# Earlier row gathers and weighings, and map products behind the value gates, in an attention and mixture-of-experts kernel

## The chip, the cores and the metric

The kernel runs on one core of one Trainium2 chip. A core has five engines with their own in-order instruction streams: PE (TensorE, matrix products; its weight loads are shown apart as PEld), DVE (VectorE), ACT (ScalarE), POOL (GpSimd) and SP (SyncE, which here only issues transfers). The metric is the device time of one execution in microseconds (us); three runs of the kernel before gave 779.08, 781.21 and 781.72 us.

## The reference

Three stages follow each other on 4 x 576 = 2304 tokens with 8 heads of 64 features.

```python
# 1 linear attention with random features, per batch and head
def phi(x):
    proj = x @ w_phi                                   # 64 -> 128
    proj = proj - max(abs(proj), axis=-1)
    return concatenate([exp(proj), exp(-proj)])        # 256 features
kv  = phi(k)^T @ v ;  z = sum(phi(k))
x   = (phi(q) @ kv) / (phi(q) @ z + 1e-6)              # -> 2304 x 512
# 2 mixture of experts, top 1 of 8, at most 576 tokens each
idx = argmax(x @ w_gate) ;  gate = softmax(x @ w_gate)[idx]
y   = relu(x[token] @ w1[e]) @ w2[e] ;  x = gate * y   # 512 -> 1024 -> 512
# 3 one dense layer on all tokens
h   = x @ w_in ;  out = (h - tanh(h)) @ w_out          # 512 -> 2048 -> 512
```

A token that finds its expert full gives a row of zeros.

## The kernel before

**Attention** works in 25 steps `s` on 18 chunks of 128 tokens. In a step the keys of chunk `s` are projected, the products of keys and values of chunk `s-1` are added (`kv_step`, PE line 347), the queries of chunk `s-5` are projected (PE line 304 into `xb`), and the outputs of an earlier chunk are formed (`num`, PE line 420). `sub` is on DVE: it takes the largest absolute value (line 312) and subtracts it (line 315); as `xb` serves keys and queries in turn, the next projection waits for line 315. `vgate` (PE line 334, result in the PSUM tile `sb`, copied by ACT at line 338) makes the part of the expert logits that comes from the values. Beside this, 13 pieces of the dense layer's weights are unpacked on ACT, DVE (lines 92 and 94) and POOL (lines 98 and 278).

**Routing** goes by groups of three chunks. `since[cs]` is the number of steps since the group's last chunk had its output formed. For the first four groups (`paced`) one step does `route1`, the next its rest, the third `prefix`, `route2` and `table`, and the fourth the products of the map: `map_mm` (PE line 576) multiplies two small tables, `ta` from DVE (line 558) and `tb` from POOL (line 548), into another part of `sb`, and `map_add` (DVE lines 581 and 583) adds them to `idc`. From `idc` the lists of rows that each expert gets are made at the end of attention.

**Experts and dense layer** work in units of 576 tokens; a unit is one expert that has tokens, and in these data three units are run. A unit has 8 steps through the expert (`ff1`, `ff2`) and then 16 steps through the dense layer: two blocks `b` of 288 tokens, eight pieces of 256 hidden features each. A dense step `s` is, on PE, `ffin` of step `s` (24 products) and `ffout` of step `s-2` (24 products). The nonlinearity (`gate`) stands between: ACT copies `ffin`'s PSUM tile `h` to `hs` (line 938) and squares it, POOL makes a mask (line 943) in the tile `AL` that `ffout` of step `s-2` still reads, DVE does the rest (lines 947 to 955, then line 931 for the low part). There is one `hs`, two tiles `h` and two `AL`.

In the dense steps of a unit the rows of the next unit are fetched. `xgather` clears one of three tiles `row` on POOL (line 860) and issues an indirect transfer from POOL's queue (line 861); `weigh` multiplies the row by its attention denominators on POOL (line 872); `xsplit` at the start of steps 8, 9 and 10 transposes it on PE (line 881, four products) and splits it into high and low parts on ACT and DVE (lines 849 and 850). Steps 11 to 13 have four transposes each too, of finished rows (`orow`, line 976). The third unit fetches for a fourth that is not run.

The order of every engine is the order in which the code is written (no scheduler moves it). In a dense step `xgather` and `weigh` come last, behind the mask of the same step:

```python
if 5 <= s <= 7:
    xgather(j + 1, s - 5)
...
if s in (7, 8, 9, 15):
    weigh()
```

Of the kernel before, what the change touches and what calls it, by code (L numbers as in the profile page):

```python
# [37 lines left out]
def build(nc, tc, ctx, qT, kT, vT, v, w_phi, w_gate, w12, win, wout, out, cap):  # L38
# [86 lines left out]
    def attention():  # L125
# [534 lines left out]
        for s in range(NCH + LAG + 2):  # L660
            i, j, jt = s, s - LAG, s - LAG - 1
            jn = jt if s < SD else jt - 1 if s > SD else -1
            kk, qq, tt = i < NCH, 0 <= j < NCH, 0 <= jt < NCH
            pc, pd = CV.get(s), CV.get(s - 1)
            since = {cs: s - (cs[-1] + LAG + 1 + (cs[-1] + LAG + 1 >= SD)) for cs in groups}
            if s == SK:
                stk.close()
                mo["alloc"]()
                qpools.append(st.enter_context(tc.tile_pool(name="qp2", bufs=1)))
            if kk:  # L670
                proj("k", i, xb if i > LAG or i % 2 == 0 else yb)
            if tt:
                trans(jt)
                qexp(jt, 0)
                qexp(jt, 1)
            if jn == NCH - 2:
                first_gather()
            for cs in maps:
                if since[cs] == 1 + 2 * (cs in paced):
                    prefix(cs)  # L680
                if since[cs] == 2 + 2 * (cs in paced) and cs in maps[:-1]:
                    map_mm(cs)
            if 0 <= i - 1 < NCH:
                kv_step(i - 1)
            if kk:
                for _ in sub("k", i):
                    pass
            bits = iter(()) if pc is None else cv_main(pc)
            next(bits, None)
            if qq:  # L690
                proj("q", j, xb)
            if i - 1 in strad:
                kv_second(i - 1)
            ke = kexp(i) if kk else iter(())
            next(ke, None)
            if pd is not None:
                cv_hi(pd)
                cv_lo(pd)
            for _ in ke:
                pass  # L700
            if qq:
                for _ in sub("q", j):
                    pass
            smalls = []
            for cs in groups:
                d = since[cs]
                if cs in paced:
                    if d == 1:
                        rgen[cs] = route1(cs)
                        smalls.append(itertools.islice(rgen[cs], 5))  # L710
                    if d == 2:
                        smalls.append(rgen[cs])
                    if d == 3:
                        smalls.append(itertools.chain(route2(cs), table(cs)))
                    if d == 4:
                        smalls.append(map_add(cs))
                elif cs in maps and d == 1:
                    smalls.append(itertools.chain(route2(cs), table(cs)))
            weave([], smalls)
            for _ in bits:  # L720
                pass
            flush()
            if 0 <= jn < NCH:
                num(jn)
            if kk:
                vgate(i)
            if CV.get(s + 1) is not None:
                cv_mag(CV[s + 1])
            for cs in groups:
                if cs not in paced and since[cs] == 0 and cs != tailg[1]:  # L730
                    weave([], [route1(cs)])
            if s + 2 < NCH:
                ldk(s + 2)
            if 0 <= j + 2 < NCH:
                ldq(j + 2)
            if pc is not None:
                cv_load(pc + NRAW)
            if s in (3, 4):
                cv_load(s - 3)
            if s + 2 < NCH:  # L740
                ldvt(s + 2)
            for c, a in vslot.get(s, []):
                if c > 1:
                    ldv(c, a)
            if 0 <= jn < NCH - NL:
                xstore([jn])
            for c in range(max(0, 4 * (s - NCH)), min(NCH, 4 * (s - NCH) + 4)):
                nc.sync.dma_start(out=out[c * P:(c + 1) * P, :].rearrange("t (a b) -> t a b", a=4),
                                  in_=zero.unsqueeze(1).to_broadcast([P, 4, P]))
            mo["after"](s)  # L750
            if jn == NCH - 2:
                xscale(NCH - 3)
# [40 lines left out]
    def experts():  # L793
# [277 lines left out]
        def unit(j, prev):  # L1071
# [64 lines left out]
            for s, (b, p) in enumerate(seq2):  # L1136
                if more and 8 <= s <= 10:
                    xsplit(s - 8)
                if 11 <= s <= 13:
                    orow(j, 0, s - 11)  # L1140
                h = ffin(b, p)
                if s == 0:
                    aq2[s] = gate(h)
                    ff2(aq.pop(n1 - 1), False, True)
                    evac_y(1)
                p2 = -1
                if s >= 2:
                    p2 = seq2[s - 2][1]
                    ffout(aq2.pop(s - 2), p2, p2 == 0, p2 == NP2 - 1)
                if s > 0:  # L1150
                    aq2[s] = gate(h, HALVES[:2] if s == n2 - 1 else HALVES[2:])
                if j == 0:

                    for k, f in enumerate(lord[LF:]):
                        if s == 2 * k:
                            late_load(f)
                        elif s == 2 * k + 1:
                            lbits[f] = late_bits(f)
                            next(lbits[f])
                            next(lbits[f])  # L1160
                        elif s == 2 * k + 2:
                            for _ in lbits[f]:
                                pass
                        elif s == 2 * k + 3:
                            late_split(f)
                if p2 == NP2 - 1:
                    evac_o(False)
                if more:
                    if s == 0:
                        use(j + 1)  # L1170
                        idload(j + 1, hs[:, 0])
                    if 5 <= s <= 7:
                        xgather(j + 1, s - 5)
                    if s == 3+WO:
                        wnext(0, 2)
                    if s == 4+WO:
                        wnext(1, 2)
                    if s == 5+WO:
                        wnext(0, 1)
                    if s == 6+WO:  # L1180
                        wnext(1, 1)
                    if s == 13:
                        xgather(j + 1, 3)
                    if s == 14:
                        xgather(j + 1, 4)
                    if s in (7, 8, 9, 15):
                        weigh()
            return [aq2[n2 - 2], aq2[n2 - 1]]

# [123 lines left out]
```

## Time and profile before

| | |
|---|---|
| runs (us) | 779.08, 781.21, 781.72 |
| the profiled execution (us) | 784.24, of which the span from first to last instruction is 782.5 |
| PE busy | 685.3 us (88%), 7148 products, mean granted clock 0.945 |
| DVE busy | 533.7 us (68%) |
| ACT busy | 431.0 us (55%) |
| POOL busy | 256.1 us (33%) |
| PE waits for `row` (line 872) before line 881 | 35.0 us in 9 |
| PE waits for `tb` and `ta` before line 576 | 12.3 us in 3, 6.9 us in 4 |

An engine's busy time says how much it worked, not whether it was waited for. The view of waits names for each idle stretch the instruction that ended it. The view by stretches gives every engine's busy time between two points of the span with PE's granted clock, where 1.00 is 2.4 GHz and half of it 1.2 GHz. In a timeline a row has its start, its duration, the instruction, and in brackets the engine's idle time ahead of it and what ended that.

### The profile page before, as it was taken

How to read it: one execution, taken by the hardware profiler on the slowest of the kernel's cores; microseconds unless marked ns; L12 is line 12 of the kernel's file. 1: busy time of each engine (PE TensorE's matmuls, PEld its weight loads, DVE VectorE, ACT ScalarE, POOL GpSimd, SP SyncE). 2: the span in 40 equal slices, each digit the busy share in tenths (PEclk: the TensorE clock that was granted, in tenths of full speed). 3: DMA queues.
4: the chain of work that ended last, by engine and by line, in shares of the span. 5: the costliest groups of instructions: out<-in, count | busy, mean ns of one | idle time of the engine just before them, and what ended most of it. 6: DMA issues, size and time to landing. Idle time of an engine off the chain costs nothing. (4 is left out here: it accounts for less than half of the span.)

```text
span 782.5 us, 17539 instructions
## 1 busy us (share of the span) xinstructions
PE 685.3 (88%) x7148; PEld 662.5 (85%) x7148; DVE 533.7 (68%) x830; ACT 431.0 (55%) x735; POOL 256.1 (33%) x227
## 2 busy tenths in 40 slices
PE   7899877967679999966999999976999999976995
PEld 6888767866569999966999999976999999976994
DVE  3689869657756767865986637745787636756783
ACT  2599767644544655644664536633664536634761
POOL 1044535342224233543461002433252002343351
PEclk9999989889968999989999999987999999989998
DMA  5987756626726630110223530000222440000111
GB/s 155 275 250 247 241 176 199 210 58 188 209 85 186 218 110 28 40 32 1 75 58 105 162 125 2 11 20 1 60 73 91 150 151 1 4 29 0 52 43 34
DMA packets 62155, 81.35 MB, mean 104 GB/s; under 512 B 25792, under 2 KB 35136, under 8 KB 60400
## 3 DMA queue, kind: packets, MB, share of 16 engines
q1 hardware_dynamic: 58736, 71.92, 29.7%
q0 software_dynamic: 2624, 8.13, 3.6%
q8 instruction: 58, 0.95, 0.5%
q14 instruction: 33, 0.27, 0.1%
q10 hardware_dynamic: 704, 0.08, 0.1%
HBM read 67.06 MB, written 13.05 MB: 102 GB/s over the span
## 5 line engine op out<-in xcount | busy, mean ns | idle before, releaser
L943 POOL TENSOR_SCALAR al<-ut 128x576 fp32r<-128x576 f32 (+1 forms) x51 | 83.1, 1629 | 200.1 <-ACT y L942 89.6
L853 PE MATMUL h<-xh,w_in_h 128*128 128x288 f32 x384 | 121.4, 316 | 0.0
L854 PE MATMUL h<-xl,w_in_h 128*128 128x288 f32 x384 | 118.9, 310 | 0.0
L855 PE MATMUL h<-xh,w_in_l 128*128 128x288 f32 x384 | 118.3, 308 | 0.0
L938 ACT COPY hs<-h 128x576 f32<-128x576 f32 (+1 forms) x51 | 31.3, 614 | 124.1 <-PE h L855 74.6
L840 DVE TENSOR_TENSOR w<-raw,w 128x512 fp32r<-128x512 f32 x98 | 67.8, 709 | 42.5 <-ACT w L835 34.7
L931 DVE TENSOR_TENSOR al<-y,ah 128x576 fp32r<-128x576 f32 (+1 forms) x51 | 38.1, 746 | 78.4 <-ACT ah L930 76.0
L835 ACT CAST w<-raw 128x512 fp32r<-128x512 f32 x98 | 58.9, 620 | 54.0 <-DMA raw<-w 22.0
L853 PEld LDWEIGHTS h<-xh,w_in_h 128*128 128x128 f32 x384 | 78.2, 204 | 0.0
L854 PEld LDWEIGHTS h<-xl,w_in_h 128*128 128x128 f32 x384 | 78.0, 203 | 0.0
L855 PEld LDWEIGHTS h<-xh,w_in_l 128*128 128x128 f32 x384 | 77.8, 203 | 0.0
L853 PE MATMUL acc<-ah,w_oa_h 128*128 128x288 f32 x240 | 71.0, 296 | 1.9 <-ACT ah L930 1.9
L854 PE MATMUL acc<-al,w_oa_h 128*128 128x288 f32 x240 | 71.1, 296 | 1.6 <-DVE al L931 1.6
L855 PE MATMUL acc<-ah,w_oa_l 128*128 128x288 f32 x240 | 70.7, 294 | 0.0
L312 DVE TENSOR_REDUCE m<-xb 128x8 f32<-128x1024 f32 x33 | 40.3, 1220 | 44.1 <-PE xb L304 44.1
L853 PE MATMUL h<-xh,w 128*128 128x288 f32 x192 | 58.9, 307 | 1.1 <-DVE al L899 1.1
L983 POOL DMA_INDIRECT out<-row,ids x18 | 20.8, 1154 | 118.7 <-DVE row L981 80.8
L347 PE MATMUL kvb<-v,kp 128*64 128x74 f32 x1280 | 53.2, 249 | 5.2 <-issue 3.1
L854 PE MATMUL h<-xl,w 128*128 128x288 f32 x192 | 57.5, 299 | 0.0
L855 PE MATMUL h<-xh,w 128*128 128x288 f32 x192 | 57.3, 299 | 0.0
L347 PEld LDWEIGHTS kvb<-v,kp 128*64 128x64 f32 x1280 | 50.0, 155 | 8.1 <-issue 4.8
L853 PE MATMUL acc<-ah,w 128*128 128x288 f32 x192 | 56.7, 295 | 0.0
(223 smaller groups left out, 1940.7 us busy)
## 6 DMA issues: line engine op xcount, KB each, us to landing
raw<-w SPq DMA_DIRECT2D x98, 256.0 KB, 2.8
raw<-win SPq DMA_DIRECT2D x8, 1024.0 KB, 7.1
raw<-wout SPq DMA_DIRECT2D x5, 1024.0 KB
k<-kT SPq DMA_DIRECT2D x18, 256.0 KB, 5.2
vt<-vT SPq DMA_DIRECT2D x18, 256.0 KB, 5.7
q<-qT SPq DMA_DIRECT2D x18, 256.0 KB, 2.5
out<-zero SPq DMA_DIRECT2D x18, 256.0 KB, 3.6
v<-v SPq DMA_DIRECT2D x16, 256.0 KB, 5.8
```

The lines of the kernel that those rows point to most:

```text
L312: nc.vector.tensor_reduce(out=m, in_=ps, axis=AX.X, op=ALU.max, apply_absolute_value=True)
L347: nc.tensor.matmul(kvb[64 * a:64 * a + 64, bank, col * NKV:col * NKV + VS], kp[i][:, 4 * g + hp, s, 64 * a:64 * a + 64], vt[:, 2 * hp + g, :],
L835: nc.scalar.copy(d[:, 0], t)
L840: eng.tensor_tensor(out=d[:, 1], in0=t, in1=d[:, 0].bitcast(F32), op=ALU.subtract)
L853: nc.tensor.matmul(o, ah, bh, start=first, stop=False, skip_group_check=True)
L854: nc.tensor.matmul(o, ah, bl, start=False, stop=False, skip_group_check=True)
L855: nc.tensor.matmul(o, al, bh, start=False, stop=last, skip_group_check=True)
L931: nc.vector.tensor_tensor(out=AL[a][:, i], in0=y2[:, i], in1=AH[a][:, i].bitcast(F32), op=ALU.subtract)
L938: nc.scalar.copy(hs[:, i], h[:, i, 0:BLK])
L943: nc.gpsimd.tensor_scalar(out=AL[a][:, i], in0=ut[:, i], scalar1=C2, scalar2=None, op0=ALU.is_gt)
L983: ins = nc.gpsimd.indirect_dma_start(out=out[:, :], out_offset=bass.IndirectOffsetOnAxis(ap=ids[j % 2][0:RCH, rc:rc + 1], axis=0), in_=r[0 ...
```

## The change

In the dense steps, the three gathers `xgather(j + 1, 0..2)` are written at steps 4 to 6 instead of 5 to 7, and their `weigh` at steps 6, 7, 8 instead of 7, 8, 9. The transposes stay at 8, 9, 10. In attention, `map_mm` of the first four groups stays in the same step but is written behind `num` and `vgate` instead of ahead of `kv_step`; `map_add` goes to the step after.

```diff
@@ attention, PE part of a step
             for cs in maps:
                 if since[cs] == 1 + 2 * (cs in paced):
                     prefix(cs)
-                if since[cs] == 2 + 2 * (cs in paced) and cs in maps[:-1]:
-                    map_mm(cs)
             if 0 <= i - 1 < NCH:
                 kv_step(i - 1)
@@ DVE part of a step
-                    if d == 4:
+                    if d == 5:
                         smalls.append(map_add(cs))
@@
             if kk:
                 vgate(i)
+            for cs in paced:
+                if since[cs] == 4:
+                    map_mm(cs)
@@ dense step of a unit
-                    if 5 <= s <= 7:
-                        xgather(j + 1, s - 5)
+                    if 4 <= s <= 6:
+                        xgather(j + 1, s - 4)
@@
-                    if s in (7, 8, 9, 15):
+                    if s in (6, 7, 8, 15):
                         weigh()
```

POOL in the dense steps of the second unit, before, from the mask of step 4 to that of step 8 (`al` is the mask, `MEMSET row` and `DMA row` are one gather, `TENSOR_TENSOR row` is one weighing):

```order
L943 TENSOR_SCALAR al_3144<-ut 128x576
L943 TENSOR_SCALAR al_3145<-ut 128x576
L860 MEMSET row_2511 96x520
L861 DMA row_2511<-xs,ids_72 96x520
L943 TENSOR_SCALAR al_3144<-ut 128x576
L860 MEMSET row_2512 96x520
L861 DMA row_2512<-xs,ids_72 96x520
L943 TENSOR_SCALAR al_3145<-ut 128x576
L860 MEMSET row_2513 96x520
L861 DMA row_2513<-xs,ids_72 96x520
L872 TENSOR_TENSOR row_2511<-row_2511 96x2x4x64
L943 TENSOR_SCALAR al_3144<-ut 128x576
```

The first weighing stands behind the mask of step 7 and the third gather. The same place of the changed kernel, again from the mask of step 4 (lines are one higher there, buffer numbers one lower):

```order
L944 TENSOR_SCALAR al_3144<-ut 128x576
L861 MEMSET row_2510 96x520
L862 DMA row_2510<-xs,ids_72 96x520
L944 TENSOR_SCALAR al_3145<-ut 128x576
L861 MEMSET row_2511 96x520
L862 DMA row_2511<-xs,ids_72 96x520
L944 TENSOR_SCALAR al_3144<-ut 128x576
L861 MEMSET row_2512 96x520
L862 DMA row_2512<-xs,ids_72 96x520
L873 TENSOR_TENSOR row_2510<-row_2510 96x2x4x64
L944 TENSOR_SCALAR al_3145<-ut 128x576
L873 TENSOR_TENSOR row_2511<-row_2511 96x2x4x64
```

Each gather and each of the three weighings now stands one mask earlier: the first weighing is behind the mask of step 6, the second behind that of step 7.

PE in step 12 of attention, the difference (`L576` is the map of chunks 0 to 2, three pairs of which one is shown; `L304` projects keys, then queries; `L420` is `num`, `L334` the value gates):

```order
 L304 MATMUL xb<-wphi,k 128x128 x8
 L381 MATMUL yb<-ident,d 128x128 x8
+L347 MATMUL kvb<-v_156,kp 64x74 x32
+L304 MATMUL xb<-wphi,q 128x128 x8
+L420 MATMUL yb<-kvs_166,qp 64x74 x32
+L334 MATMUL sb<-wgb,vt 64x16 x8
 L576 LDWEIGHTS ta
 L576 MATMUL sb<-tb,ta 96x98
...
-L347 MATMUL kvb<-v_156,kp 64x74 x32
-L304 MATMUL xb<-wphi,q 128x128 x8
-L420 MATMUL yb<-kvs_166,qp 64x74 x32
-L334 MATMUL sb<-wgb,vt 64x16 x8
```

The rest of the step's products have moved ahead of the map; the map itself stands last in its step.

DVE, the sum of the first map (`idc<-sb`) in steps 12 and 13, the difference (`m` and `d` are `sub` of the queries):

```order
 L312 TENSOR_REDUCE m<-xb 128x8
 L315 TENSOR_TENSOR d<-xb,m 128x1024
-L581 COPY idc<-sb 96x98
 L448 TENSOR_SCALAR r<-dl 128x24
 L449 RECIPROCAL r<-r 128x24
...
 L312 TENSOR_REDUCE m<-xb 128x8
 L315 TENSOR_TENSOR d<-xb,m 128x1024
+L581 COPY idc<-sb 96x98
 L472 TENSOR_TENSOR cand<-lg,mx 128x24
 L474 TENSOR_TENSOR cand<-cand,e_122 128x24
```

The copy went one step later, to the same place behind `sub` of the queries.

## Rows read from the trace of the kernel before

**Rows 1.** Waits of PE: instruction and releaser, us in total, times, longest.

```profile
PE h L881 <- POOL row L872: 35.0, 9, 6.0
PE sb L576 <- POOL tb L548: 12.3, 3, 4.7
PE sb L576 <- DVE ta L558: 6.9, 4, 3.9
```

**Rows 2.** Dense stretches: us, busy of PE, PEld, DVE, ACT, POOL (count); PEclk, DMA share, GB/s.

```profile
337.02:373.45 36.43, 24.34 (x158) 23.86 (x158) 20.06 (x24) 16.58 (x30) 10.51 (x8) 0.86 0.04 11
513.94:553.05 39.11, 27.64 (x157) 27.17 (x157) 17.79 (x23) 14.36 (x26) 10.93 (x8) 0.78 0.02 6
692.18:728.30 36.12, 24.65 (x158) 24.16 (x157) 17.80 (x23) 14.37 (x26) 10.93 (x8) 0.86 0.02 7
553.05:573.40 20.35, 20.35 (x158) 20.34 (x157) 19.16 (x27) 13.83 (x24) 8.43 (x6) 1.00 0.28 82
```

**Rows 3.** Timeline of PE at step 8 of units 1 and 2.

```profile
343.03 0.90 PE L881 MATMUL h<-ident,row 96*128 96x96 f32 x4 [6.01 <-POOL row L872]
...
519.33 0.90 PE L881 MATMUL h<-ident,row 96*128 96x96 f32 x4 [5.39 <-POOL row L872]
```

**Rows 4.** Timeline of POOL: step 6 of unit 1; steps 6 to 8 of unit 2.

```profile
332.37 1.65 POOL L943 TENSOR_SCALAR al<-ut 128x576 fp32r<-128x576 f32 x1 [0.18 <-ACT ut L939]
...
507.59 1.82 POOL L943 TENSOR_SCALAR al<-ut 128x576 fp32r<-128x576 f32 x1 [2.05 <-ACT ah L930]
...
513.97 2.21 POOL L943 TENSOR_SCALAR al<-ut 128x576 fp32r<-128x576 f32 x1 [2.35 <-ACT y L942]
...
518.22 1.06 POOL L872 TENSOR_TENSOR row<-row 96x512 f32<-96x512 f32 x1
...
530.75 1.32 POOL L872 TENSOR_TENSOR row<-row 96x512 f32<-96x512 f32 x1
```

**Rows 5.** Transfers by line, from issue to landing: the gathers, last number the median.

```profile
row<-xs,ids POOLq DMA_INDIRECT x23, 3.8
```

**Rows 6.** Timeline of DVE: line 954 in steps 7 and 8 of unit 2.

```profile
516.51 0.75 DVE L954 TENSOR_TENSOR th<-hs,th 128x576 f32<-128x576 f32 x1
...
531.09 1.60 DVE L954 TENSOR_TENSOR th<-hs,th 128x576 f32<-128x576 f32 x1
```

**Rows 7.** Timeline of ACT: copy of `h` in step 7 of unit 1.

```profile
336.80 0.64 ACT L938 COPY hs<-h 128x576 f32<-128x576 f32 x1 [1.77 <-DVE th L954]
```

**Rows 8.** Stretches of attention, columns as in rows 2: steps 12, 15, 18, 20, 21.

```profile
94.90:109.98 15.08, 10.86 (x191) 10.05 (x187) 9.63 (x17) 7.84 (x10) 5.32 (x4) 0.77 0.65 216
...
131.07:146.98 15.91, 11.44 (x192) 10.55 (x188) 9.79 (x11) 8.93 (x13) 7.38 (x4) 0.79 0.72 214
...
165.69:180.40 14.71, 9.68 (x159) 9.04 (x155) 5.22 (x11) 4.65 (x9) 4.90 (x4) 0.77 0.11 36
...
185.26:190.19 4.93, 4.49 (x93) 4.21 (x93) 3.71 (x11) 2.33 (x4) 0.60 (x3) 1.00 0.51 154
190.19:196.66 6.47, 4.73 (x91) 4.20 (x92) 4.63 (x12) 2.63 (x5) 2.09 (x4) 1.00 1.00 294
```

**Rows 9.** Timeline of PE in attention: steps 12 and 15.

```profile
95.99 1.09 PE L381 MATMUL yb<-ident,d 128*128 128x128 f32 x8
...
101.13 4.21 PE L347 MATMUL kvb<-v,kp 128*64 128x74 f32 x64
...
141.77 1.88 PE L304 MATMUL xb<-wphi,q 64*128 64x128 f32 x16
```

**Rows 10.** Timeline of DVE in attention: `sub` of the keys in steps 12 and 15.

```profile
99.99 1.23 DVE L315 TENSOR_TENSOR d<-xb,m 128x1024 f32<-128x1024 f32 x1
...
135.64 1.23 DVE L315 TENSOR_TENSOR d<-xb,m 128x1024 f32<-128x1024 f32 x1
```

**Rows 11.** Timeline of POOL and of ACT in step 12: `tb`, copy of the value gates.

```profile
100.07 0.68 POOL L548 TENSOR_TENSOR tb<-lt,tokv 128x294 bf16<-128x294 bf16 x1
...
110.10 0.22 ACT L338 COPY v<-sb 128x64 f32<-128x64 f32 x1 [0.44 <-PE sb L334]
```

## The prediction

> **What bounds the kernel now.** I read the waits of PE first, since PE is busy for 88% of the span. Two of its waits are large, and the change touches both: the transposes of the next unit's rows wait for the weighing on POOL, 35.0 us in nine waits, and the map products wait for their tables, 12.3 us in three and 6.9 us in four [rows 1]. Then I cut the span into stretches to see what a wait costs beside its own length.
>
> In the three units the stretch from the end of PE's step 7 to the start of step 11 takes 36.43, 39.11 and 36.12 us [rows 2]. It begins at the transpose's start less its wait, 343.03 - 6.01 = 337.02 and 519.33 - 5.39 = 513.94 [rows 3]. Steps 11 to 13 of unit 2 are the same amount of PE work (158 rows; four transposes and 48 products in each step) and take 20.35 us, with PE busy throughout and the clock granted in full [rows 2]. In the slow stretches the granted clock is 0.78 to 0.86, so PE also ran at half clock, 1.2 GHz, for a while behind its waits. The rest of the dense steps and the expert steps show no such wait in rows 1, so PE sets the end there, and what it loses in these stretches it never gets back.
>
> Why the transposes are late is in POOL's rows. The mask of step `s` writes the tile that `ffout(s-2)` reads, so it starts when PE ends the step: mask 7 starts at 513.97, while PE reached the transposes at 513.94. Behind it, in the same queue, stand the clearing, the third gather and the first weighing, which ends at 518.22 + 1.06 = 519.28 [rows 4]; PE goes on at 519.33. Steps 9 and 10 repeat this with mask and weighing alone.
>
> In attention, steps 12, 15 and 18 take 15.08, 15.91 and 14.71 us with a granted clock of 0.77 to 0.79; step 21 takes 6.47 us, the step ahead of it 4.93 [rows 8]. In step 12 PE is done with the transposes at 95.99 + 1.09 = 97.08, and the key-value products behind the map begin only at 101.13 and take 4.21 us at half clock [rows 9].
>
> **The gathers and weighings.** Nothing is added or removed; three gathers and three weighings per unit go up one mask in POOL's queue. From the start of the mask to the end of the weighing behind it are 519.28 - 513.97 = 5.31 us [rows 4]. In unit 2 the new place is behind mask 6: 507.59 + 5.31 = 512.90, and PE wants the row at 513.94, so it is 1.0 us early. The second weighing, behind mask 7, ends at about 513.97 + 2.21 + 1.32 = 517.5 [rows 4], and PE wants it one step (20.35 / 3 = 6.8 us) after 513.94; that is 3.2 us early, and the third likewise. Unit 3 repeats unit 2. In unit 1 mask 6 starts at 332.37 [rows 4], so the weighing ends at 337.68 against 337.02: 0.7 us of wait stay there. The transfers hide: a gather lands 3.8 us after its issue [rows 5], and its weighing stands two steps behind it, as before. Step 4 gets a clearing and an issue, step 7 is rid of them.
>
> The full gain is the stretches at the pace of steps 11 to 13: 36.43 + 39.11 + 36.12 - 3 x 20.35 = 50.6 us [rows 2]; 35.0 of it are the waits themselves, 15.6 the half clock behind them. What may be late next is the chain of the nonlinearity, which had slack while PE stood still. In unit 1 it runs behind PE: the copy of step 7's `h` starts at 336.80 [rows 7], when PE is nearly done with step 7. The squaring that follows is a second read of that tile, which I estimate at the copy's 0.64 us, so the tile comes free at about 338.1. `ffin(8)` goes into it, and with 0.7 us of wait and some 0.4 for the transposes it would begin at 338.1. That just fits.
>
> A weighing also slows DVE: line 954 takes 0.75 us alone and 1.60 beside the weighing of 530.75 [rows 4, 6], which is 0.85 more. Before, most of these fell into time in which PE waited anyway; that cover is gone. Bounds: a loss of nothing, or of 9 x 0.85 = 7.7 us if each of nine weighings lengthens PE's step by all of it. I take 1.5 us in unit 1 (0.7 of wait and one such delay) and 0.6 each in units 2 and 3, because the chain is followed by a full `ffin` before `ffout` needs its result. That leaves 50.6 - 2.7 = 48 us.
>
> The Trainium skill says of this ("SBUF — State Buffer", section "Who interferes with whom") that DVE and GpSimd share one pair of ports as an exclusive lock, and that the one that comes second blocks for the whole instruction instead of sharing. The 1.60 against 0.75 agrees. By that rule alone the loss would be the upper bound of 7.7 us, and the sum would come out 5 us worse; it is the first rival below.
>
> **The map products.** In step 12 PE no longer waits for `tb`, which is done at 100.75 [rows 11]. The key-value products start at 97.08 instead of 101.13. The query projection behind them then meets the next wait: it writes the tile that DVE reads until 99.99 + 1.23 = 101.22 [rows 10]. It began where the half-clock products ended, at about 105.3 [rows 9], so the gain is 4.0 us. In step 15 DVE is done at 136.87, and PE began at 141.77 [rows 9, 10]: 4.9 us. Step 18 has no new keys and no value gates, so nothing holds the projection: the wait is that of 4.7 us [rows 1], the key-value products go back to about half of their 4.2 us, the projection behind them gets some 0.7 back, less 0.3 for the map itself: 7.0 us. Step 21 falls to the length of step 20: 6.47 - 4.93 = 1.5 us [rows 8]. Together 17.4.
>
> At its new place the map waits for something new: its weight load stands behind ACT's copy of the value gates out of the same tile. That copy waits 0.44 us for the gates and takes 0.22 [rows 11], so PE stands for some 0.4 us in two steps, and with it the next step's key projection, for which DVE waits. The sum `idc` moves to the next step, where the value gates wait for it as they did in their own step; that nets to nothing, and its bound either way is a fraction of a microsecond per map. Bounds for this part: 0, if another engine takes over, and 19.2 + 5, all waits [rows 1] and the half clock behind them (some 2 us in each of the first three). I take 17.
>
> **The sum.** 48 + 17 = 65. The profiled execution took 784.24 us (span 782.5), so 719.2; the median run, 781.21, lies 3.0 lower, and I predict 716 us.
>
> **Rivals.**
> 1. The nonlinearity becomes the bound in steps 8 to 10. For it: unit 1's chain is already behind PE [rows 7], and weighings lengthen DVE's work [rows 6]. Against: steps 11 to 13 with 19.16 us of DVE work in 20.35 keep PE full [rows 2], and in steps 8 to 10 DVE had only 17.8 to 20.1. Price 7.7 us: 716 + 7.7 - 2.7 = 721. With a lag in which PE also waits for a tile `h`, once per unit and for about 1 us (the copy and the squaring), 724.
> 2. Attention gives nothing back: DVE is the next bound (9.6 to 9.8 us of work in steps 12 and 15, rows 8), and what is won is lost in waits for the unpacking of weights before attention ends. Against: step 18 has 5.22 us of DVE work in 14.71. Price 17: 733.
> 3. The change moves the waits but does not remove them: the first weighing of each unit is still late, since its margin is 1.0 us at best. If all three firsts keep 5.4 us of wait and about 2 us of half clock, 22 us stay: 738.
> 4. Slower. The weighing stands ahead of mask 7 now, and POOL waits in order; should the gathered rows land late, mask 7 is held back and with it `ffout`. From gather to weighing are two steps of 513.97 - 507.59 = 6.4 us [rows 4], against a landing of 3.8 [rows 5]. The point from which it decides: to eat 65 us in nine weighings, each must hold the mask by over 7 us, so landings of 20 us and more, and then the time is 782 to 790. Nothing in the rows is near it.
>
> **How the numbers follow.** Forecast 0.72, with its own range of 709 (all 50.6 and 21 us) to 722; rival 1 0.10, rival 2 0.11, rival 3 0.04, rival 4 0.02, and 0.01 for a time within 0.3% of before, which is 2.3 us and about what a measurement can tell. All but the last two are faster: 0.97. The range goes from 708, just under the best sum, to 734, which takes in rivals 1 and 2.
>
> **What would show it.** Right: PE's wait for line 872 falls from 35 us to under 3, and only unit 1's first transposes still wait; the three stretches take 20.5 to 22 us at a granted clock of 1.00; no map product waits for `tb`; steps 12, 15, 18 take about 11, 11 and 7.5 us. Wrong: waits of PE for the copy or the squaring of `h`, or for the low part from line 931, in steps 8 to 10 (rival 1); waits of PE for DVE's `d` longer than 2 us in steps 12 and 15, or a half clock there, or attention ending at the same time as before (rival 2); a wait of POOL for the landing of `row` ahead of a mask (rival 4).

## The result and the profile after

The changed kernel takes 719.33 us (median of four runs, 717.26 to 720.24), the kernel before 781.47 on the same chip: a ratio of 0.9195, 95% interval 0.9149 to 0.9241. The forecast was 716 us, and 709 to 722 for the likeliest case. Another set of six runs gave 717.78, ratio 0.9187 [0.9162, 0.9213]. The profiled execution is the one of 717.26 us, 67.0 less than the 784.24 before.

The first line of the profile's page after, and its line of busy times. PE's busy time fell by 28.5 us with the same 7148 products: less of the work ran at half clock.

```profile
span 715.4 us, 17537 instructions
...
PE 656.8 (92%) x7148; PEld 636.5 (89%) x7148; DVE 537.2 (75%) x830; ACT 431.1 (60%) x735; POOL 256.4 (36%) x227
```

Waits of PE after, columns as in [rows 1] (line numbers from about 725 on are one higher):

```profile
PE xb L304 <- DVE d L315: 11.7, 11, 2.2
PE sb L576 <- DVE ta L558: 5.8, 3, 3.9
...
PE h L854 <- ACT ut L940: 1.4, 1, 1.4
...
PE sb L576 <- ACT v L338: 1.0, 2, 0.5
...
PE h L882 <- POOL row L873: 0.3, 1, 0.3
```

The 35.0 us in nine waits for the weighing are 0.3 in one; the 12.3 us for `tb` are gone. Of the 6.9 us for `ta`, 5.8 stay: they are ahead of the maps of the last groups, which the change does not move. The dense stretches of [rows 2], from the end of step 7 to the start of step 11, are now:

```profile
319.16:341.31 22.15, 20.50 (x156) 20.31 (x157) 18.66 (x24) 15.76 (x29) 7.59 (x6) 1.00 0.03 8
481.62:501.83 20.21, 20.21 (x158) 20.21 (x157) 17.40 (x22) 14.34 (x27) 7.35 (x5) 1.00 0.00 1
640.81:661.02 20.21, 20.21 (x158) 20.20 (x157) 17.41 (x22) 14.34 (x27) 7.35 (x5) 1.00 0.01 2
```

In units 2 and 3 PE is busy for all of the stretch, at the full 2.4 GHz. POOL's timeline at the first weighing of unit 2, the place of [rows 4], shows why:

```profile
479.50 1.06 POOL L873 TENSOR_TENSOR row<-row 96x512 f32<-96x512 f32 x1
481.80 1.66 POOL L944 TENSOR_SCALAR al<-ut 128x576 fp32r<-128x576 f32 x1 [1.25 <-issue]
```

The weighing ends at 480.56, 1.06 us before PE wants the row at 481.62 (1.0 was predicted). In unit 1 PE still waits, twice:

```profile
319.46 0.55 PE L882 MATMUL h<-ident,row 96*128 96x96 f32 x4 [0.30 <-POOL row L873]
...
321.36 0.40 PE L854 MATMUL h<-xh,w_in_h 128*128 128x288 f32 x1 [1.36 <-ACT ut L940]
```

First for the row, then for the tile `h` that ACT is still squaring. The squaring is late because ACT's copy of `h` ahead of it waits for DVE, and DVE's operation stood beside the weighing in its new place (318.34 to 319.40). Before, no weighing stood there. DVE's operation for step 6 of unit 1, before and after:

```profile
335.96 0.75 DVE L954 TENSOR_TENSOR th<-hs,th 128x576 f32<-128x576 f32 x1
```

```profile
318.10 1.93 DVE L955 TENSOR_TENSOR th<-hs,th 128x576 f32<-128x576 f32 x1
```

In attention, stretches after by step: 12, 13, 15, 16, 18, then 19 and 20 together, then 21. Columns as in [rows 8], which has steps 12, 15, 18 and 21 of before:

```profile
92.26:103.11 10.85, 8.48 (x191) 7.77 (x187) 9.63 (x16) 8.15 (x12) 5.22 (x4) 1.00 0.85 287
103.11:113.42 10.31, 8.37 (x186) 7.63 (x184) 9.31 (x14) 7.84 (x10) 4.50 (x2) 1.00 0.55 167
124.23:134.68 10.45, 8.56 (x192) 7.77 (x188) 9.99 (x8) 9.07 (x14) 7.15 (x4) 1.00 0.85 252
134.68:144.80 10.12, 8.37 (x186) 7.62 (x184) 9.15 (x14) 7.80 (x10) 4.75 (x3) 1.00 0.81 261
...
154.22:161.28 7.06, 6.80 (x158) 6.27 (x156) 5.32 (x11) 4.52 (x8) 3.65 (x4) 1.00 0.26 77
161.28:174.03 12.75, 9.07 (x120) 8.34 (x118) 9.61 (x21) 4.64 (x7) 2.17 (x4) 0.73 0.64 188
174.03:178.89 4.86, 4.69 (x94) 4.23 (x92) 4.47 (x10) 3.04 (x6) 2.09 (x4) 1.00 0.99 287
```

Steps 13, 16 and 19 with 20 of the kernel before:

```profile
109.98:119.53 9.55, 8.15 (x188) 7.57 (x184) 8.55 (x13) 7.54 (x11) 3.78 (x2) 1.00 0.58 175
146.98:155.56 8.58, 8.15 (x189) 7.57 (x185) 7.67 (x11) 7.54 (x11) 3.80 (x2) 1.00 0.62 187
180.40:190.19 9.79, 6.68 (x117) 6.07 (x117) 8.14 (x21) 4.80 (x8) 0.91 (x4) 1.00 0.63 187
```

Steps 12, 15, 18 and 21 gained 4.2, 5.5, 7.7 and 1.6 us; steps 14 and 17, which lie between these rows, 0.7 each. Steps 13, 16 and 19 with 20 gave back 0.8, 1.5 and 3.0. From the start of step 12 to the end of step 21 that makes 196.66 - 94.90 = 101.76 before against 178.89 - 92.26 = 86.63: 15.1 us. With the dense stretches (111.66 - 62.57 = 49.1) and 2.6 us by which step 12 began earlier, in code that was not touched, the two profiled executions' difference is accounted for to 0.2 us: 66.8 of 67.0. Those 2.6 us belong to the execution: over all the profiles told of here step 12 began between 91.1 and 94.9 us, with the map moved or not (94.31 in a second profile of the changed kernel). The end of attention neither gains nor loses: PE now waits 3.6 us for a weighing there (line 621) where it waited 1.6 us for ACT, but from the end of step 21 to the first product of the experts it takes 37.5 us, 37.6 before.

### The profile page after: what moved, and what is told of

Its sections match the earlier page's. It is cut to its first block, busy times and chain, and to the rows that moved or that the text cites. A ratio compares the mean times of both kernels' runs of the same rounds, so it can differ in the third digit from the quotient of the medians.

```text
span 715.4 us, 17537 instructions
## 1 busy us (share of the span) xinstructions
PE 656.8 (92%) x7148; PEld 636.5 (89%) x7148; DVE 537.2 (75%) x830; ACT 431.1 (60%) x735; POOL 256.4 (36%) x227
## 4 chain that ended last, share of the span: by engine, by line
PE 61%; DVE 16%; DMA 10%; ACT 7%; issue 3%; POOL 2%; SPq 0%; ACTq 0%; DVEq 0%; POOLq 0%
PE h L854 9%; PE acc L855 9%; PE acc L856 9%; PE acc L854 9%; PE h L856 9%; PE h L855 9%; DMA out<-row,ids 6%; DVE d L315 3%; DVE m L312 3%; PE xb L304 2%; PE kvb L347 1%; DMA raw<-win 1%; PE kvb L420 1%; POOL w_in_l L278 1%; ACT a L85 1%
## 5 line engine op out<-in xcount | busy, mean ns | idle before, releaser
L854 PE MATMUL h<-xh,w_in_h 128*128 128x288 f32 x384 | 115.0, 299 | 1.4 <-ACT ut L940 1.4
L855 PE MATMUL h<-xl,w_in_h 128*128 128x288 f32 x384 | 113.3, 295 | 0.0
L856 PE MATMUL h<-xh,w_in_l 128*128 128x288 f32 x384 | 113.0, 294 | 0.0
L854 PEld LDWEIGHTS h<-xh,w_in_h 128*128 128x128 f32 x384 | 72.0, 188 | 1.5 <-ACT ut L940 1.5
L856 PEld LDWEIGHTS h<-xh,w_in_l 128*128 128x128 f32 x384 | 72.3, 188 | 0.0
L855 PEld LDWEIGHTS h<-xl,w_in_h 128*128 128x128 f32 x384 | 72.1, 188 | 0.0
L932 DVE TENSOR_TENSOR al<-y,ah 128x576 fp32r<-128x576 f32 (+1 forms) x51 | 41.3, 810 | 33.8 <-ACT ah L931 30.3
L854 PE MATMUL acc<-ah,w 128*128 128x288 f32 x192 | 56.7, 295 | 0.0
L856 PE MATMUL acc<-ah,w 128*128 128x288 f32 x192 | 56.6, 295 | 0.0
L855 PE MATMUL acc<-al,w 128*128 128x288 f32 x192 | 56.5, 294 | 0.0
```

The source lines that it names most:

```text
L854: nc.tensor.matmul(o, ah, bh, start=first, stop=False, skip_group_check=True)
L855: nc.tensor.matmul(o, ah, bl, start=False, stop=False, skip_group_check=True)
L856: nc.tensor.matmul(o, al, bh, start=False, stop=last, skip_group_check=True)
L932: nc.vector.tensor_tensor(out=AL[a][:, i], in0=y2[:, i], in1=AH[a][:, i].bitcast(F32), op=ALU.subtract)
```

## The experiments

**Dense part alone.** Gathers and weighings moved, the map as before.

```diff
-                    if 5 <= s <= 7:
-                        xgather(j + 1, s - 5)
+                    if 4 <= s <= 6:
+                        xgather(j + 1, s - 4)
...
-                    if s in (7, 8, 9, 15):
+                    if s in (6, 7, 8, 15):
```

> The dense part of the change alone: gathers at steps 4 to 6, weighings at 6, 7, 8; the map products stay ahead of the key-value products. My theory (the dense and the attention part add up, and the dense one is the stretches of steps 8 to 10 alone): 49 us less than the kernel before, 781.5 - 49 = 732, with the three stretches at 22.2, 20.2 and 20.2 us and PE's three waits for tb of 4 to 5 us still there. Rival (the two parts share a limit, so that one alone gives more or less than its part): under 726 or over 738.

Measured: 731.61 us against 781.41, ratio 0.9353 [0.9302, 0.9403], so -49.8. Its stretches of units 1 and 2:

```profile
333.05:356.72 23.67, 22.02 (x156) 21.83 (x157) 19.45 (x25) 16.45 (x30) 7.73 (x6) 0.93 0.03 9
496.36:516.57 20.21, 20.21 (x158) 20.20 (x157) 17.42 (x22) 14.33 (x27) 7.34 (x5) 1.00 0.00 1
```

The term of 48 stands. Unit 1 here lost 1.5 us more than in the changed kernel, to half clock behind its two waits (granted clock 0.93 against 1.00).

**Map part alone.** `map_mm` and `map_add` as in the change, the dense steps as before.

```diff
-                if since[cs] == 2 + 2 * (cs in paced) and cs in maps[:-1]:
-                    map_mm(cs)
...
-                    if d == 4:
+                    if d == 5:
                         smalls.append(map_add(cs))
...
+            for cs in paced:
+                if since[cs] == 4:
+                    map_mm(cs)
```

> The map part of the change alone: map products behind the value gates, their sum one step later; gathers and weighings as before. The trace of the changed kernel has the experts begin 17.9 us earlier, but step 12, the first that the change touches, already begins 2.6 us earlier there, in code that is the same. My theory: those 2.6 us are the execution's and not the change's, so this gives 15 us: 766, and steps 12 to 22 are 15 us shorter than before whatever the start does. Rival (all 17.9 are the change's): 763 or less. The nine waits for the weighing stay at 35 us.

Measured: 769.07 us, ratio 0.9808 [0.9755, 0.9862]: -12.3 between medians, -15.0 by the ratio, with an interval of -10.8 to -19.1, which takes in the 15.1 of the traces and the 17 predicted. In its trace steps 12 to 21 take 86.41 us, 15.4 less than the 101.76 before, as my theory had it. The waits for `row` stay:

```profile
PE h L882 <- POOL row L873: 35.0, 9, 6.0
```

The two parts add up as far as can be measured: 49.8 + 12.3 = 62.1, and the whole change brought 781.47 - 719.33 = 62.1. That the tenths agree is luck, since the interval of the map part alone is 8 us wide; by the ratios the parts are 50.6 and 15.0 and the whole is 62.9.

**Weighings alone.** Gathers stay at steps 5 to 7; only `if s in (6, 7, 8, 15)` is changed.

> Only the weighings go up, to steps 6, 7, 8; the gathers stay at steps 5 to 7. From the gather behind mask 5 to the weighing behind mask 6 is one step of 6.4 us, and a gather lands 3.8 us after its issue. My theory (the weighing's place behind the mask is what made PE wait, the transfer was hidden anyway): 733, within 2 us of the run with both moves, and POOL waits for no landing for more than 1 us. Rival (the earlier gather is needed): each weighing waits for its rows, the mask behind it is held back, and the gain falls by 9 x 2 us or more: 750 and over.

Measured: 733.68 us, ratio 0.9365 [0.9315, 0.9415]. Unit 2:

```profile
497.72:518.40 20.68, 20.40 (x158) 20.19 (x157) 17.96 (x23) 14.66 (x27) 9.43 (x7) 1.00 0.04 10
```

That is 0.47 us more than with the gathers moved too. The weighing's place did the work, and one step between gather and weighing is enough for the landing of 3.8 us [rows 5]: none of the nine weighings at steps 6 to 8 waits for it in this trace.

**Gathers alone.** Only `if 4 <= s <= 6: xgather(j + 1, s - 4)` is changed.

> Only the gathers go up, to steps 4 to 6; the weighings stay at 7, 8, 9. The clearing and the issue of the third gather (some 2.1 us with the gap) no longer stand between mask 7 and the first weighing. My theory: each unit's first wait falls from 5.4 or 6.0 us to some 3.3, the other two stay at 3.04: 6 us less in waits, up to 3 us more where the clock is then granted earlier: 773 to 776. Rival (PE waits for the transfer, not for POOL's queue): all nine waits fall below 1 us and the time is 735.

Measured: 775.58 us (ten runs, 773.57 to 784.3), ratio 0.9923 [0.989, 0.9955]. PE's waits:

```profile
PE h L881 <- POOL row L872: 29.4, 9, 4.0
```

The three first waits lost what the third gather had cost ahead of the weighing (6.01 and twice 5.39 us became 3.96, 3.61 and 3.60); the other six stayed at 3.04. POOL's queue, not the transfer, made the rows late.

**Filling the wait.** The kernel before with 20 more products on PE ahead of each transpose of steps 8 to 10; their results are overwritten unused.

```diff
+        def fill(n):
+            h = hp_[cnt["h"] % len(hp_)]
+            for _ in range(n):
+                nc.tensor.matmul(h[:, 0, 0:BLK], w_in_h[:, 0, 0:P], xh[1][:, 0, :], start=True, stop=True,
+                                 skip_group_check=True)
...
                 if more and 8 <= s <= 10:
+                    fill(20)
                     xsplit(s - 8)
```

> The kernel before with 20 more products on PE (2.7 us at full clock, results not used) ahead of the transposes in steps 8, 9 and 10 of each unit, so that PE works through most of its nine waits for the weighing, which stay as they are. In the kernel before, the three stretches of steps 8 to 10 are 4.0, 7.3 and 4.3 us longer than waits and work at full clock make them. My theory (that is PE at half clock behind its waits): those 15.6 us go, up to 3 us of them may stay behind the three long first waits, of which 2.7 us are still idle: 766 to 769, and the granted clock of the stretches is 0.95 or more. Rival (the longer products come from something else that runs then, such as the weighing or the nonlinearity): no gain, 781 or a little more.

Measured: 769.07 us, ratio 0.9829 [0.9795, 0.9863], -12.7. Its stretches, from the first added product of step 8:

```profile
335.45:369.90 34.45, 30.36 (x219) 29.65 (x217) 20.11 (x24) 16.74 (x30) 10.51 (x8) 0.95 0.05 12
508.88:541.19 32.31, 28.85 (x218) 28.14 (x217) 17.88 (x23) 14.47 (x27) 10.92 (x8) 1.00 0.03 7
680.34:714.18 33.84, 30.36 (x218) 29.66 (x217) 17.89 (x23) 14.46 (x27) 10.93 (x8) 0.95 0.02 7
```

The rows come no earlier, yet the three stretches take 100.6 us instead of 111.66 [rows 2], with the granted clock at 0.95 to 1.00 instead of 0.78 to 0.86. So the half clock behind the waits was a cost of its own: 11.1 of the 15.6 us that the prediction gave it came back when PE was merely kept busy, and unit 2, at full clock throughout, got 6.8.

**Map one step later.** The kernel before, with `map_mm` at its old place in the code (ahead of `kv_step`) but a step later.

```diff
-                if since[cs] == 2 + 2 * (cs in paced) and cs in maps[:-1]:
+                if since[cs] == 5 and cs in paced:
                     map_mm(cs)
...
-                    if d == 4:
+                    if d == 5:
```

> The kernel before with the map products at their old place ahead of the key-value products, but one step later (their sum also one step later); the dense part as before. My theory (what cost time was that the map stood ahead of tb; any place behind tb does): as the map part alone, 769, within 3 us, no wait for tb, and no wait for ACT's copy of the value gates. Rival (it matters that PE has the rest of the step ahead of the map): waits of PE for the tables remain in these steps and the time is 775 or more.

Measured: 766.31 us, ratio 0.9814 [0.9783, 0.9845], -15.5 (14.5 by the ratio). Any place behind `tb` does it; the copy of the value gates is not waited for here.

**Map between `num` and the value gates.** The changed kernel with the two last blocks of a step exchanged, which takes the new wait for ACT's copy (0.50 and 0.51 us, twice) away.

```diff
+            for cs in paced:
+                if since[cs] == 4:
+                    map_mm(cs)
             if kk:
                 vgate(i)
-            for cs in paced:
-                if since[cs] == 4:
-                    map_mm(cs)
```

> The changed kernel with the map products between the output products and the value gates, so that they do not stand behind ACT's copy of the gates. In the changed kernel that costs two waits of 0.5 us. My theory: those two go, tb is done 3 us ahead, nothing takes their place: 1 us less than the changed kernel run beside it. Rival (DVE is next in those steps and its wait grows by the same): no difference within 0.3 us in the length of steps 12 and 15.

Measured: 718.23 us, ratio 0.9195 [0.9169, 0.922]. The changed kernel was run again beside it:

> The changed kernel again, beside the one with the map ahead of the value gates: 719.3, and a start of step 12 that differs by up to 4 us from execution to execution, in code that the change does not touch.

It took the 717.78 us told above. Steps 12 with 13 and 15 with 16 took 21.26 and 20.56 us in the edited kernel, 21.27 and 20.54 in the changed one: what step 12 gains by the edit (12.12 against 12.47) step 13 gives back (9.14 against 8.80), and so do 15 and 16. The new wait was real, but it cost nothing. These pairs of steps hardly vary: in six profiles that have the map moved behind the value gates or `num` and all of DVE's work in these steps they took 21.16 to 21.35 and 20.54 to 20.57 us, whether or not step 12 had half clock.

**DVE's part made lighter.** Is DVE what holds these pairs? The changed kernel, with one operation of the unpacking of weights left out in four steps.

```diff
-    def cv_bits(t, a, m):
+    def cv_bits(t, a, m, bits=True):
...
+        if bits:
             nc.vector.scalar_tensor_tensor(out=a, in0=t[:, :, 0], scalar=29, in1=a,
...
+            ... cvm.pop(i), i not in [CV[s] for s in (12, 13, 15, 16)])
```

> The changed kernel, with the second operation of DVE's unpacking of the weights (the shift and or, 1.22 us) left out in attention steps 12, 13, 15 and 16, so that DVE has 2.4 us less work in each of the two pairs of steps. Four pieces of the dense layer's weights are then not the reference's. In the changed kernel the pairs take 21.2 and 20.6 us, with DVE busy for 19.0 and 19.1. My theory, that DVE is the bound of these pairs once the map no longer holds PE up, expects the pairs at 18.8 and 18.2 us (less each by 2.4), with PE's waits for d before the query projections still there but shorter; the time then 3 to 5 us under that of the changed kernel, some 713 to 716 us. The rival, that the pairs are held by something else (PE's own order, the copy of the value gates, the transfers), expects them at 20.5 to 21.3 us as before and the time at 717 to 720 us, with DVE idle for longer.

Measured: 720.41 us, ratio 0.9209 [0.9166, 0.9252]. The pairs did not shorten; they took 21.66 and 20.91, with DVE's busy time up:

```profile
92.51:114.17 21.66, 18.44 (x376) 16.98 (x372) 19.44 (x28) 15.70 (x21) 9.79 (x7) 0.92 0.65 221
125.71:146.62 20.91, 16.99 (x375) 15.43 (x371) 19.48 (x20) 16.81 (x24) 11.86 (x7) 1.00 0.87 264
```

The reading fits neither theory: the second pair is where the rival had it, but the first is longer than either said, and DVE is not idle for longer. In the changed kernel the multiplication on POOL (line 98) waits 2.96 us for the operation that was left out. Now it started at once, beside small operations of DVE. Timelines of DVE and of POOL in this run (lines one higher):

```profile
103.74 1.90 DVE L459 TENSOR_TENSOR lgx<-dl,r 128x192 f32<-128x192 f32 x1
...
114.23 2.07 DVE L475 TENSOR_TENSOR cand<-cand,e 128x24 f32<-128x24 f32 x1
```

```profile
103.29 2.13 POOL L99 TENSOR_TENSOR a<-a,m 128x1024 f32<-128x1024 f32 x1
...
114.12 2.13 POOL L99 TENSOR_TENSOR a<-a,m 128x1024 f32<-128x1024 f32 x1
```

In the changed kernel the two take 0.36 and 0.18 us. Each now ends within 0.3 us of POOL's, so 1.22 us left out came back as 1.54 and 1.89. The second of them stands in step 14, behind the pair. Steps 16 and 17 repeat both (1.90 and 2.07 us), and steps 14 and 17 took 0.7 us more each than in the changed kernel.

**POOL's multiplication left out too.** As before, with `if bits:` ahead of line 98 as well.

> As the run before it (the changed kernel without the shift and or on DVE in attention steps 12, 13, 15 and 16), and POOL's multiplication behind it (line 98, 2.14 us) left out in those steps too; four pieces of the dense layer's weights are then not the reference's. In the run before, that multiplication no longer waited for DVE and so ran beside two small operations of DVE, which took 1.90 and 2.07 us instead of 0.36 and 0.18, and the pairs of steps took 21.7 and 20.9 us, no less than in the changed kernel. If DVE's time is what bounds the pairs, they now take 18.8 and 18.2 us (2.4 less each) and the time is 713 to 717 us. If something else holds them (PE's own order, the copies, the transfers), they stay at 20.5 to 21.3 us and the time at 717 to 720 us, with DVE idle for longer.

Measured: 717.19 us, ratio 0.9151 [0.9115, 0.9188], which can't be told from the changed kernel. The pairs:

```profile
93.97:114.28 20.31, 16.86 (x376) 15.40 (x372) 18.09 (x28) 15.74 (x21) 7.61 (x5) 1.00 0.78 255
124.94:145.09 20.15, 16.98 (x375) 15.48 (x371) 16.62 (x20) 16.19 (x24) 11.06 (x5) 1.00 0.85 266
```

They lost 0.9 us (from 21.16) and 0.4 (from 10.45 + 10.12), not the 2.4 that I expected. One part of that was a slip: of two operations left out in a pair, only the first stands ahead of projections of the pair; the second belongs to the step behind it. Steps 12 to 17 together took 59.95 us, against 61.96 and 62.08 in the two profiles of the changed kernel: 2.0 us less, of 4.9 left out. The other part is what came next. PE's waits in step 15 of this run:

```profile
127.56 2.27 PE L349 MATMUL kvb<-v,kp 128*64 128x74 f32 x64 [0.28 <-DMA v<-v]
...
132.03 2.31 PE L422 MATMUL yb<-kvs,qp 128*64 128x74 f32 x64 [1.11 <-ACT qp L389]
135.57 0.34 PE L578 MATMUL sb<-tb,ta 128*96 128x98 bf16 x3 [0.80 <-ACT v L340]
```

In step 15 the wait for `d` was 1.30 us in the changed kernel and is gone here; waits for ACT's `qp` and `v` and for a transfer have taken its place. The pairs came out as neither side expected (18.8 and 18.2, or 20.5 to 21.3), but in these two runs they moved by more than they vary between profiles, up and down with DVE's busy time. So DVE holds them in the changed kernel, and ACT and the transfers stand close behind it.

**Steps 19 and 20: no subtraction on POOL.** In all seven profiles so far with the map moved these two steps took 11.8 to 12.8 us; in four of five without, 9.8 to 10.0, and in the fifth, the dense part alone, 11.3. After, POOL's subtraction of the last unpacked weight lies beside the first operation of DVE's routing. Rows of POOL, then of DVE after:

```profile
160.49 2.36 POOL L278 TENSOR_TENSOR w_oa_l<-a,w_oa_h 128x1024 fp32r<-128x1024 f32 x1 [0.52 <-ACT w_oa_h L275]
```

```profile
161.05 1.83 DVE L448 TENSOR_SCALAR r<-dl 128x24 f32<-128x24 f32 x1
```

That operation took 0.32 us in the same place before. The changed kernel without the subtraction:

```diff
         def cv_lo(i):
+            if i == CV[17]:
+                nc.gpsimd.memset(pieces[i][2].bitcast(F32), 0.0)
+                return
```

> The changed kernel, with POOL's subtraction for the last of the 13 unpacked pieces (line 278, 2.36 us, in attention step 18) replaced by a clearing that reads nothing; the low part of that one piece of weights is then zero. In every kernel with the map moved, steps 19 and 20 took 11.8 to 12.8 us, against 9.8 to 10.0 in four of five kernels with the map at its old place (11.3 in the fifth). My theory: that subtraction now lies beside the first operation of DVE's routing (line 448: 1.83 us, 0.32 before), which makes d 1.5 us late, and PE's longer wait (3.7 us, 2.7 before) is followed by half clock in step 20. It expects line 448 at 0.2 to 0.4 us, PE's wait ahead of step 20 down by 1 to 1.5 us, and steps 19 and 20 at 9.5 to 10.8 us; the time 1.5 to 3 us less, 715 to 717. The rival: the wait comes from DVE's order (the routing ahead of the queries' subtraction), which was hidden before because PE reached step 19 late; the collision is then a small part, and steps 19 and 20 stay at 11.3 to 12.8 us and the time at 717 to 720.

Measured: 716.1 us (714.15 to 719.95), ratio 0.9177 [0.9133, 0.922]: by the time alone no difference. PE in steps 19 and 20 of the changed kernel, then of this one:

```profile
167.11 1.94 PE L381 MATMUL yb<-ident,d 128*128 128x128 f32 x8 [3.68 <-DVE d L315]
...
169.08 2.08 PE L304 MATMUL xb<-wphi,q 64*128 64x128 f32 x16
171.09 3.00 PE L420 MATMUL kvb<-kvs,qp 128*64 128x74 f32 x64
```

```profile
167.36 1.94 PE L384 MATMUL yb<-ident,d 128*128 128x128 f32 x8 [2.68 <-DVE d L318]
...
169.33 1.73 PE L307 MATMUL xb<-wphi,q 64*128 64x128 f32 x16
```

Line 448 is down to 0.17 us and PE's wait to the 2.68 that it had before. Step 19 takes 4.83 us (162.53 to 167.36) against 5.83 after and 4.86 before: the collision is worth 1.0 us. Step 20 takes 6.38 against 6.92 after and 4.93 before; its first products still run at half clock (1.94 us in both rows, 1.06 in the kernel before). Both steps take 11.21 us, between the theory (9.5 to 10.8) and the rival (11.3 to 12.8). The collision is a third of the 3.0 us lost; step 20's half us less is no more than it varies with the map moved (5.96 to 6.92 us in the seven profiles). The rest is clock, and it is not the map's alone: step 20 of the run with only the dense part changed shows it too.

```profile
181.42:187.41 5.99, 5.99 (x92) 5.55 (x93) 3.70 (x11) 1.94 (x2) 0.59 (x3) 0.72 0.62 184
```

PE's wait ahead of it was 3.11 us there. In the four other profiles with the map at its old place it was 2.68 to 2.89, with a granted clock of 1.00 behind it, but the run without the subtraction has 2.68 too, and 0.75. So the length of that one wait does not tell the clock.

**The same, by order.** The changed kernel with DVE's last unpacking operation of step 17 ahead of the routing's.

```diff
+            if s == 17:
+                for _ in bits:
+                    pass
             weave([], smalls)
             for _ in bits:
                 pass
```

> The changed kernel, with DVE's last unpacking operation of step 17 (line 94) ahead of the routing's operations of that step instead of behind them, so that POOL's multiplication, ACT's cast and POOL's subtraction of the last piece come some 2 us earlier and the subtraction ends before line 448 of step 18 begins. Nothing is left out. If the collision of that subtraction with line 448 is what makes steps 19 and 20 long, line 448 takes 0.2 to 0.4 us, steps 19 and 20 take 9.5 to 10.8 us and the time is 715 to 717 us; POOL's multiplication may lengthen an operation of step 17's routing by up to 2 us, which DVE's idle 1.5 us in step 18 covers. If the wait comes from DVE's order, steps 19 and 20 stay at 11.3 to 12.8 us and the time at 717 to 720.

Measured: 721.27 us, ratio 0.9246 [0.9215, 0.9277], so no gain and rather a loss. The subtraction came no earlier: ahead of it ACT's cast stands in ACT's queue behind the exponentials and copies of step 18, and it started at 162.38, beside line 448 at 163.60 (1.19 us). In step 17 the moved operation, 1.97 us long beside another subtraction of POOL's, made PE wait instead, with half clock behind:

```profile
154.59 0.64 PE L334 MATMUL sb<-wgb,vt 128*64 128x16 f32 x16 [2.32 <-DVE pos L514]
...
156.32 3.74 PE L347 MATMUL kvb<-v,kp 128*64 128x74 f32 x64
```

No version tried beats the changed kernel by more than a measurement can tell.

## Why the prediction was right, and where it was off

**The cause.** Right, and shown by parts: the weighing's place in POOL's queue made the rows late, moving it alone is worth 47.7 us where the dense part alone is worth 49.8, and moving the gathers alone 5.8.

**The dense term**, 48 us: 49.1 in the traces, 49.8 alone. Its parts held as well: the margin of the first weighing (1.06 against 1.0), the half clock as a cost of its own (the filling run), and unit 1's rest, 22.15 - 20.35 = 1.8 against the 1.5 taken. The rest was put together otherwise, so the closeness of its sum is partly luck: the wait for the row was 0.30 and not 0.7, and "that just fits" was wrong for the tile `h`, for which PE waited 1.36 us. The forecast took the copy of step 7's `h` where it was before, 0.2 us ahead of the end of PE's step; with DVE's operation lengthened by the weighing it came 1.0 us behind it. Units 2 and 3 were charged 0.6 each and lost nothing.

**Rival 1** (the nonlinearity becomes the bound) came in unit 1 alone: the wait of 1.36 us for the squaring is the sign named for it. In units 2 and 3 it did not come, though its mechanism is there. In unit 2 the chain now runs behind PE: ACT's copy of `h` waits for DVE instead of for PE, as this row of ACT in step 8 shows, while PE stays busy for 20.21 of 20.21 us. The full step of `ffin` between `h` and `ffout` covers it.

```profile
486.82 0.64 ACT L939 COPY hs<-h 128x576 f32<-128x576 f32 x1 [1.99 <-DVE th L955]
```

**The map term**, 17.4 taken as 17: 15.1 in the traces, 12.3 and 15.5 between medians (15.0 and 14.5 by the ratios) in two kernels timed with the map alone moved. The single steps came out as predicted or better (10.85, 10.45 and 7.06 us against 11, 11 and 7.5), except that step 12 took 12.47 in the second profile, with the half clock that the prediction named as a sign against it; step 13 gave that back. The upper bound was too wide: it counted all 6.9 us of waits for `ta`, of which only the 1.31 of step 21 belong to a map that moves. What failed in the sum is that the steps between were taken to stay as they were:

| steps | predicted gain, us | in the traces |
|---|---|---|
| 12 and 13 | 4.0 | 24.63 - 21.16 = 3.5 |
| 15 and 16 | 4.9 | 24.49 - 20.57 = 3.9 |
| 18 | 7.0 | 7.7 |
| 21 | 1.5 | 1.6 |
| 14 and 17 | 0 | 1.4 |
| 19 and 20 | 0 | -3.0 |

In steps 13 and 16, 0.7 us is only moved (the wait for `idc`, 0.50, as foreseen, and 0.2 of PE's time). The rest of the shortfall in these pairs is the new wait for the copy and, in step 16, a wait for `d` of 1.25 us that was 0.42 before: DVE had worked on while PE stood waiting for the map, and that lead is gone (DVE is busy for 9.15 us in step 16 now, 7.67 before). Steps 19 and 20 are the largest item: 1.0 us of it is the collision, shown by the run without the subtraction; why the clock fell in step 20 here and not in the profile before is open. Rival 2 is thus there in part, with 2 us of its 17.

**The new wait** for ACT's copy of the value gates was foreseen at 0.4 us in two steps; it is 0.50 and 0.51, and taking it away is worth nothing.

**Rivals 3 and 4** did not come: only unit 1's first weighing is still late, by 0.30 us, and POOL's waits for the landing of `row`, 9.8 us in all (8.3 before), stand ahead of none of the nine weighings that moved.

**The sum.** 65 us forecast, 62.1 between medians. The 3.0 us from the profiled execution to the median was a property of one run: the profiled execution after lies 2.1 under its own median. By its terms the dense part brought 1 to 2 us more than forecast and the map 2 to 5 less; the two errors partly cancel, and 719.33 is 3.3 over 716.

## What to carry to other kernels

Where an engine's instructions are in order, look at what stands ahead of the one that is waited for: here a small multiplication stood behind a mask that could start only when PE was already in need of the result, and one place earlier in the queue was worth 50 us. Price a wait on PE with the clock that is lost behind it (here 15.6 us on 35.0, of which 11.1 were shown to be the clock's), and price the removal of waits in a pipeline over two steps, not one, since the other engines catch up during a stall and give the next step a lead that goes with it.

## What the runs showed of the hardware that was not expected

The same wait of PE does not always cost the clock. In step 12 of the changed kernel the 64 products behind a wait of 1.87 us for `d` ran at full clock in one profile:

```profile
98.51 1.16 PE L304 MATMUL xb<-wphi,q 64*128 64x128 f32 x16 [1.87 <-DVE d L315]
99.60 2.32 PE L420 MATMUL yb<-kvs,qp 128*64 128x74 f32 x64
```

In the second profile of the same kernel they did not, behind 1.97 us:

```profile
100.66 1.16 PE L304 MATMUL xb<-wphi,q 64*128 64x128 f32 x16 [1.97 <-DVE d L315]
101.75 3.83 PE L420 MATMUL yb<-kvs,qp 128*64 128x74 f32 x64
```

That step is 1.6 us longer (12.47 against 10.85), and the next 1.5 shorter (8.80 against 10.31), since DVE gains its lead again.

A DVE operation of 0.18 us took 2.07 beside one of POOL and ended with it. The Trainium skill says so ("SBUF — State Buffer", section "Who interferes with whom"): DVE and GpSimd share a pair of ports as a lock held for the whole instruction. Here the trace agrees: the operation ended 0.05 us after POOL's. What the runs add is that work left out on DVE can come back whole where it had held POOL off.
